# The queries' factors of a decayed attention kernel, taken as the reciprocal of its first scan

## The chip, the cores and the metric

The program runs on one core of a Trainium2 chip. The core has a matrix engine (TensorE, PE in the profile, its weight loads PEld), a vector engine (VectorE, DVE), a scalar engine (ScalarE, ACT), a general engine (GpSimd, POOL) and a queue processor (SyncE, SP), and each runs its own list of instructions in order. They meet through semaphores. On-chip memory is SBUF (128 partitions) and PSUM, into which the matrix engine writes. The metric is the time of one execution on the device, in microseconds. Less is better.

## The reference

Two parts follow each other. The first is a linear attention whose state decays by a factor `alpha` of its own for every key dimension; the second routes each token to one of eight experts.

```python
# q, k, v, alpha: (4, 8, 768, 48) = batch, heads, tokens, head size; alpha between 0.8 and 1.0
for t in range(S):
    state = alpha[:, :, t, :, None] * state + k[t] outer v[t]      # D x D per head
    y[:, :, t] = q[t] applied to state
x = y as (3072 tokens, 384)
logits = x @ w_gate + modality_bias[modality_id]
e_idx = argmax(logits);  gate_w = softmax(logits)[e_idx]
out[token] = gate_w * (relu(x @ w1[e_idx]) @ w2[e_idx])             # 384 -> 1024 -> 384
```

## The kernel before

**Attention in chunks.** The 4 x 768 tokens are cut into 24 chunks of 128 tokens (six a batch). Inside a chunk the recurrence is turned into matrix products: with P(t) the product of all decays after token t up to the chunk's end, each key is multiplied by P(t) and each query by 1/P(t). The product over the whole chunk, A, carries the state from one chunk to the next. Two heads share a tile, so that four pairs (`NP`) lie side by side.

**The decays, lines 225 to 242.** `turn_decay` turns a chunk's alpha with four transposes on TensorE (L222) and copies them to `X` (L227, on ACT but for the first chunk). `X` has four stretches of 128 decays, with a zero column between them (`SEG` = 129). `decay` then runs four VectorE instructions. L235 scans `X` backwards, 516 columns, `G = G * X + DR`; `DR` is 1 at the start of each stretch and 0 elsewhere, so `G` holds the products P(t), and A at columns `1::SEG`. L239 puts A, kept from below by `AFLOOR` = 1e-30, into `amin`. L240 takes its reciprocal, four columns, into `DF`. L241 scans `X` forwards, `Fw = Fw * X + DF`, and so gives the factors 1/P(t) as 1/A times the decays up to t. `amin` is read once, at the end of attention (`out_of_range`, L665), to see if a general way of computing is needed (it is not with these inputs).

**What uses them.** `scale_k` (L257) multiplies the turned keys by `G` into `kh`; `scale_q` (L263) the turned queries by `Fw` into `qh`. `scores` (L272) multiplies `kh` and `qh` on TensorE, ACT copies the result to `scT` (L276), POOL masks it (L277). `keys` turns `kh` back (L286, copied to `knat` by ACT). `combine` multiplies the state `S` by A (`t1`, L299, shown as `t`), copies it in halves to `UB` on ACT (L302), makes `kv` = keys by values (L308), adds it to the state (L311; L313 where a batch begins), and forms the output `y` (L321 from the state, L323 from the scores).

**The order.** The loop at L764 is a software pipeline: in step s it turns the decays of chunk s, scales the keys and queries of chunk s-1, makes the scores of s-2, combines s-3, writes out s-4. Routing of finished groups of tokens is spread over the steps. From step 4 TensorE keeps the order of the program (`pin`); on the other engines a planner that simulates the program chooses the order of the instructions, subject to what they depend on. On ACT the two copies to `UB` are placed ahead of the next step's copy to `X`. PSUM tiles named `tr` have three buffers, used in turn by the three input transposes, `keys` and `rows`.

**Experts.** After attention 12 tiles of 256 tokens run through the experts, plus partial ones (`slot`, `half`), with float32 split in two parts (L863, L865) and three products for each (L891 to L893, L914 to L916).

Of the kernel before, what the change touches and what calls it, by code (L numbers as in the profile page):

```python
# [8 lines left out]
F32 = mybir.dt.float32  # L9
# [5 lines left out]
ALU = mybir.AluOpType  # L15
# [6 lines left out]
P = 128  # L22
B, H, S, D = 4, 8, 768, 48
NC = S // P
NP = H // 2
SEG = P + 1
DM = H * D
E = 8
F = 1024
# [17 lines left out]
AFLOOR = 1.0e-30  # L47
# [5 lines left out]
def attention_moe(ctx: ExitStack, tc: tile.TileContext, q, k, v, alpha, mid, wg, mb, w1, w2, out):  # L53
    nc = tc.nc
    vec, act, pool, pe, sp = nc.vector, nc.scalar, nc.gpsimd, nc.tensor, nc.sync
# [7 lines left out]
    ac = actx.enter_context(tc.tile_pool(name="ac", bufs=1))  # L63
    sb = actx.enter_context(tc.tile_pool(name="sb", bufs=2))
# [10 lines left out]
    for i in range(NB):  # L75
        for n, val in (("a", 1.0), ("k", 0.0), ("q", 0.0)):
            t = ac.tile([P, H, 64], F32, name=f"nat_{n}{i}")
# [4 lines left out]
    for i in range(NV):  # L82
        t = ac.tile([P, H, 64], F32, name=f"vt{i}")
# [11 lines left out]
    st = {}  # L95
# [49 lines left out]


    DR = ac.tile([P, NP * SEG + 1], F32, name="DR")
    vec.memset(DR, 0.0)
    vec.memset(DR[:, SEG :: SEG], 1.0)
    X, DF, UB = [], [], []  # L150
    for i in range(2):
        t = ac.tile([P, NP * SEG + 1], F32, name=f"X{i}")
        vec.memset(t[:, 0 :: SEG], 0.0)
        X.append(t)
        t = ac.tile([P, NP * SEG], F32, name=f"DF{i}")
        vec.memset(t, 0.0)
        DF.append(t)
        t = ac.tile([P, NP, 2, 64], F32, name=f"UB{i}")
        vec.memset(t, 0.0)
        UB.append(t)  # L160
# [3 lines left out]
    amin = ac.tile([P, NU, NP], F32, name="amin")  # L164
# [51 lines left out]
    def seg(t, lo):  # L216
        return t.rearrange("p (a b) -> p a b", b=SEG)[:, :, lo : lo + P]

    def trans(i, n):
        p = ps.tile([P, NP, P], F32, name="tr", bufs=3)  # L220
        for j in range(NP):
            pin(pe.transpose(p[:, j], nat[n, i % NB][:, 2 * j : 2 * j + 2].rearrange("p a b -> p (a b)"), ident))  # L222
        return p
# [5 lines left out]
            mark["X"] = turned  # L229

    def decay(i):
        x, d = X[i % 2], DF[i % 2]
        Fw = sb.tile([P, NP * SEG], F32, name="Fw", bufs=3)
        G = sb.tile([P, NP * SEG + 1], F32, name="G", bufs=4)
        vec.tensor_tensor_scan(  # L235
            G[:, 1:][:, ::-1], x[:, 1:][:, ::-1], DR[:, 1:][:, ::-1], 0.0, op0=ALU.mult, op1=ALU.add
        )
        ac1 = amin[:, i]
        vec.tensor_scalar(ac1, G[:, 1::SEG], AFLOOR, None, op0=ALU.max)  # L239
        vec.reciprocal(d[:, 0::SEG], ac1)  # L240
        vec.tensor_tensor_scan(Fw, x[:, :-1], d, 0.0, op0=ALU.mult, op1=ALU.add)  # L241
        st[i, "G"], st[i, "F"] = G, Fw

    def guard(i):
# [15 lines left out]
    def scale_q(i):  # L260
        qh = sb.tile([P, NP, P], F32, name="qh", bufs=3)
        pq = trans(i, "q")
        vec.tensor_tensor(qh, pq, seg(st[i, "F"], 1), op=ALU.mult)  # L263
        st[i, "q"] = qh

    def scores(i):
# [497 lines left out]
    for s in range(NU + 3):  # L764
# [14 lines left out]
        if 0 <= s - 1 < NU:  # L779
            scale_q(s - 1)  # L780
        if s < NU:
            decay(s)
# [262 lines left out]
```

## Time and profile before

| what | value |
|---|---|
| runs | 430.09, 429.88, 425.59 us; median 429.88 |
| the profiled execution's own time | 424.6 us |
| its span in the trace | 422.9 us |
| mean granted TensorE clock | 0.984 |
| attention's decays run from | 6.3 us (first L235) to 152.8 us (end of the last L241) |
| VectorE instructions | 546, of which 48 are the long scans |

The span runs from the first to the last instruction. In the views, a row of the groups gives line, engine, operation, output and inputs with their shapes, the count, the busy time in all, the mean of one in ns, and the idle time ahead of them with what ended it. In a timeline row the first two numbers are start and length in us, and the bracket holds the idle time ahead and its releaser. A row of waits gives the total, the number and the longest. Consecutive VectorE instructions overlap by some hundredths of a microsecond, so the distance between starts is what one adds to the queue.

### The profile page before, as it was taken

To read this page: it belongs to the slowest core of one execution; us is meant where nothing else is said; L and a number is where in the kernel's file an instruction comes from. 1 tells how busy PE (TensorE), PEld (TensorE's weight loads), DVE (VectorE), ACT (ScalarE), POOL (GpSimd) and SP (SyncE) were. 2 spreads that over 40 slices of the span, in tenths; PEclk is the share of its full clock that TensorE was granted. 3 is DMA by queue.
4 is the path that set the end of the run, shared out by engine and by line. 5 is a ranking of instruction groups with operands and counts; after the bars stand their busy time and mean duration, and the time that the engine had idled before them with its cause. 6 is when DMAs were issued, how large, how long until landed. Compare 5 with 4: busy or idle time off the path is not lost. (4 is left out here: it accounts for less than half of the span.)

```text
span 422.9 us, 9633 instructions
## 1 busy us (share of the span) xinstructions
PE 384.9 (91%) x3659; PEld 356.4 (84%) x3659; DVE 275.4 (65%) x546; ACT 236.3 (56%) x441; POOL 133.0 (31%) x175
## 2 busy tenths in 40 slices
PE   3988998999999888889899999999999999999590
PEld 2777887888778776769799999999999999999590
DVE  6878679777888973488299567565675656622040
ACT  3577677668576555347287556556565565532220
POOL 9222121212212233403557524443352431410100
PEclk9999999999999999999999999999999999999886
DMA  7999688588484087504999966686666865300270
GB/s 147 211 196 215 149 177 167 116 170 185 115 176 108 37 297 265 189 20 153 387 312 370 321 215 212 200 296 205 208 206 205 294 208 170 115 19 21 71 279 6
DMA packets 134489, 78.37 MB, mean 185 GB/s; under 512 B 103809, under 2 KB 121278, under 8 KB 134424
## 3 DMA queue, kind: packets, MB, share of 16 engines
q1 hardware_dynamic: 130328, 67.72, 57.0%
q0 software_dynamic: 4096, 9.85, 6.1%
q8 instruction: 33, 0.54, 0.5%
q14 instruction: 32, 0.26, 0.2%
HBM read 68.10 MB, written 9.65 MB: 184 GB/s over the span
## 5 line engine op out<-in xcount | busy, mean ns | idle before, releaser
L865 DVE TENSOR_TENSOR w2L<-w2r,w2H 128x768 fp32r<-128x768 f32 x52 | 49.0, 957 | 54.1 <-ACT w2H L863 54.1
L891 PE MATMUL tr<-xH,w1H 128*128 128x256 f32 x264 | 75.2, 286 | 0.6 <-issue 0.4
L892 PE MATMUL tr<-xL,w1H 128*128 128x256 f32 x264 | 74.8, 284 | 0.4 <-issue 0.4
L893 PE MATMUL tr<-xH,w1L 128*128 128x256 f32 x264 | 74.6, 283 | 0.3 <-issue 0.3
L277 POOL TENSOR_SCALAR_AFFINE_SELECT scT<-scT 128x512 f32<-128x512 f32 x48 | 32.4, 693 | 115.0 <-ACT scT L276 114.9
L914 PE MATMUL sc<-w2H,hH 128*128 128x384 f32 x192 | 64.4, 338 | 0.0
L915 PE MATMUL sc<-w2L,hH 128*128 128x384 f32 x192 | 63.9, 335 | 0.0
L833 POOL DMA_INDIRECT out_dram<-os,odx x24 | 28.4, 1185 | 111.8 <-ACT os L919 60.9
L916 PE MATMUL sc<-w2H,hL 128*128 128x384 f32 x192 | 62.5, 335 | 0.0
L863 ACT CAST w2H<-w2r 128x768 fp32r<-128x768 f32 x52 | 42.5, 835 | 35.6 <-PE sc L916 29.6
L865 DVE TENSOR_TENSOR w1L<-w1r,w1H 128x768 fp32r<-128x768 f32 x44 | 41.7, 959 | 16.9 <-ACT w1H L863 16.3
L891 PEld LDWEIGHTS tr<-xH,w1H 128*128 128x128 f32 x264 | 50.4, 191 | 1.3 <-issue 1.3
L892 PEld LDWEIGHTS tr<-xL,w1H 128*128 128x128 f32 x264 | 50.5, 191 | 1.0 <-issue 0.9
L863 ACT CAST w1H<-w1r 128x768 fp32r<-128x768 f32 x44 | 36.0, 835 | 26.5 <-PE tr L892 22.2
L893 PEld LDWEIGHTS tr<-xH,w1L 128*128 128x128 f32 x264 | 50.6, 192 | 0.0
L898 DVE SCALAR_TENSOR_TENSOR hL<-tr,hH 128x512 fp32r<-128x512 f32 x46 | 31.5, 686 | 16.6 <-ACT hH L895 13.5
L654 POOL DMA_INDIRECT gg<-gd,idx x26 | 31.5, 1213 | 20.6 <-ACT os L919 8.8
L914 PEld LDWEIGHTS sc<-w2H,hH 128*128 128x128 f32 x192 | 36.1, 188 | 0.5 <-issue 0.5
L895 ACT ACTIVATE hH<-tr 128x512 fp32r<-128x512 f32 x46 | 27.2, 593 | 16.5 <-PE tr L893 9.0
L915 PEld LDWEIGHTS sc<-w2L,hH 128*128 128x128 f32 x192 | 36.1, 188 | 0.0
L916 PEld LDWEIGHTS sc<-w2H,hL 128*128 128x128 f32 x192 | 35.9, 188 | 0.0
L323 PE MATMUL y<-scT,vt 128*64 128x128 f32 x384 | 35.9, 273 | 0.0
(224 smaller groups left out, 750.6 us busy)
## 6 DMA issues: line engine op xcount, KB each, us to landing
w1r<-in_moe_w_dram SPq DMA_DIRECT2D x28, 768.0 KB
w2r<-in_moe_w_dram SPq DMA_DIRECT2D x28, 768.0 KB
nat_a<-in_alpha_dram SPq DMA_DIRECT2D x24, 192.0 KB
nat_k<-in_k_dram SPq DMA_DIRECT2D x24, 192.0 KB
nat_q<-in_q_dram SPq DMA_DIRECT2D x24, 192.0 KB
vt<-in_v_dram SPq DMA_DIRECT2D x24, 192.0 KB
xd<-xs SPq DMA_DIRECT2D x24, 192.0 KB
xg<-xd,idx POOLq DMA_INDIRECT x26
```

What stands on the lines that cost most here:

```text
L277: pool.affine_select(s, s, [[0, NP], [1, P]], ALU.is_ge, 0.0, base=0, channel_multiplier=-1)
L323: pin(pe.matmul(y[r, j], vt[:, 2 * j + g], sc[g][:, j], start=(c == 0), stop=True))
L654: pool.indirect_dma_start(gg[i % NX][:, u : u + 1], None, gd[0:rows], ix, bounds_check=rows - 1, oob_is_err=False)
L863: act.copy(hi, src)
L865: vec.tensor_tensor(lw, src, hi.bitcast(F32), op=ALU.subtract)
L891: pe.matmul(hp[:, z], wH[:, d, fs], xH[:, d], start=(d == 0), stop=False)
L892: pe.matmul(hp[:, z], wH[:, d, fs], xL[:, d], start=False, stop=False)
L893: pe.matmul(hp[:, z], wL[:, d, fs], xH[:, d], start=False, stop=(d == ND - 1))
L898: mark[f"h{j}L"] = vec.scalar_tensor_tensor(hL, hp, 0.0, hH.bitcast(F32), op0=ALU.max, op1=ALU.subtract)
L914: pe.matmul(op, hH[:, z, us], wH[:, z], start=(f == 0), stop=False)
L915: pe.matmul(op, hH[:, z, us], wL[:, z], start=False, stop=False)
L916: pe.matmul(op, hL[:, z, us], wH[:, z], start=False, stop=(f == NF - 1))
```

## The change

The second scan, the small maximum and the small reciprocal go. The first scan now has a maximum as its second operation, with `DR` holding `AFLOOR` in place of 0, so that the floor is kept inside the scan (`G = max(G * X, DR)`; the zero column of `X` and the 1 in `DR` still start each stretch). One reciprocal over all 4 x 128 products gives the queries' factors. The copy of A to `amin` is made by POOL. The two `DF` tiles and their memsets go; `Fw` has 512 columns in place of 516.

```diff
     DR = ac.tile([P, NP * SEG + 1], F32, name="DR")
-    vec.memset(DR, 0.0)
+    vec.memset(DR, AFLOOR)
     vec.memset(DR[:, SEG :: SEG], 1.0)
-    X, DF, UB = [], [], []
+    X, UB = [], []
...
-        t = ac.tile([P, NP * SEG], F32, name=f"DF{i}")
-        vec.memset(t, 0.0)
-        DF.append(t)
...
     def decay(i):
-        x, d = X[i % 2], DF[i % 2]
-        Fw = sb.tile([P, NP * SEG], F32, name="Fw", bufs=3)
+        x = X[i % 2]
+        Fw = sb.tile([P, NP, P], F32, name="Fw", bufs=3)
         G = sb.tile([P, NP * SEG + 1], F32, name="G", bufs=4)
         vec.tensor_tensor_scan(
-            G[:, 1:][:, ::-1], x[:, 1:][:, ::-1], DR[:, 1:][:, ::-1], 0.0, op0=ALU.mult, op1=ALU.add
+            G[:, 1:][:, ::-1], x[:, 1:][:, ::-1], DR[:, 1:][:, ::-1], 0.0, op0=ALU.mult, op1=ALU.max
         )
-        ac1 = amin[:, i]
-        vec.tensor_scalar(ac1, G[:, 1::SEG], AFLOOR, None, op0=ALU.max)
-        vec.reciprocal(d[:, 0::SEG], ac1)
-        vec.tensor_tensor_scan(Fw, x[:, :-1], d, 0.0, op0=ALU.mult, op1=ALU.add)
+        vec.reciprocal(Fw, seg(G[:, 1:], 1))
+        pool.tensor_copy(amin[:, i], G[:, 1::SEG])
         st[i, "G"], st[i, "F"] = G, Fw
...
-        vec.tensor_tensor(qh, pq, seg(st[i, "F"], 1), op=ALU.mult)
+        vec.tensor_tensor(qh, pq, st[i, "F"], op=ALU.mult)
```

## The prediction

> **What bounds the kernel now.** I read the busy time by stretch first, to find the stage that the change lies in and what fills it.
>
> ```profile
> 10.00:150.00 140.00, 130.23 (x1712) 110.94 (x1711) 114.76 (x248) 93.42 (x209) 30.15 (x46) 1.00 0.72 154
> 150.00:210.00 60.00, 52.61 (x542) 44.97 (x542) 35.09 (x129) 27.83 (x54) 21.28 (x22) 1.00 0.61 221
> 210.00:390.00 180.00, 180.00 (x1288) 179.77 (x1287) 113.66 (x146) 105.77 (x165) 69.39 (x58) 1.00 0.63 213
> ```
>
> The columns are the length, then busy time of PE, PEld, DVE, ACT and POOL, the granted clock, the DMA share and GB/s. From 10 to 150 us attention runs: PE is busy 130.2 of 140 us, VectorE 114.8, and so 25.2 us of VectorE and 9.8 us of PE are free. From 210 to 390 us TensorE is busy without a gap in the experts, which start from what attention leaves; there a later start is a later end. So a microsecond that attention gains or loses is, near enough, one of the total. The stage's price is set by its steps, one for each chunk, and next I look at what they wait for.
>
> ```profile
> ACT UB L302 <- DVE t L299: 24.2, 19, 2.7
> PE tr L286 <- ACT X L227: 6.1, 9, 1.6
> ACT X L227 <- PE tr L222: 5.9, 10, 1.4
> ```
>
> ACT stands still 19 times, 24.2 us in all, until VectorE has `t`. PE then waits for the copy of `X` that follows the `UB` copies on ACT; only 10 of the 23 `X` copies wait for PE's transposes. One step shows the ring:
>
> ```profile
> 96.99 1.22 DVE L235 TENSOR_TENSOR_SCAN G<-X,DR 128x516 f32<-128x516 f32 x1
> 98.13 0.67 DVE L263 TENSOR_TENSOR qh<-tr,Fw 128x512 f32<-128x512 f32 x1
> 98.71 0.16 DVE L239 TENSOR_SCALAR amin<-G 128x4 f32<-128x4 f32 x1
> 98.91 0.18 DVE L240 RECIPROCAL DF<-amin 128x4 f32<-128x4 f32 x1
> 99.12 1.23 DVE L241 TENSOR_TENSOR_SCAN Fw<-X,DF 128x516 f32<-128x516 f32 x1
> 100.27 0.33 DVE L313 COPY S<-kv 128x192 f32<-128x192 f32 x1
> 100.64 0.59 DVE L299 TENSOR_TENSOR t<-S,G 128x192 f32<-128x192 f32 x1
> 101.27 0.71 ACT L302 COPY UB<-t 64x192 f32<-64x192 f32 x2 [0.46 <-DVE t L299]
> 102.01 0.58 ACT L227 COPY X<-tr 128x512 f32<-128x512 f32 x1
> 102.65 1.22 DVE L235 TENSOR_TENSOR_SCAN G<-X,DR 128x516 f32<-128x516 f32 x1
> ```
>
> Scan `G`, `qh`, the three instructions for `Fw`, `S`, `t`; then ACT's `UB`, `X`; then the next scan `G`. Each starts within 0.1 us of the end of the one ahead: `UB` ends at 101.98 and `X` starts at 102.01, `X` ends at 102.59 and the scan starts at 102.65. The step is 5.66 us long, and in steps of this kind what is added between L235 and L299 on VectorE lengthens it by its full size, though VectorE has free time elsewhere.
>
> **The change part by part.** *Removed.* From the start of L239 (98.71) to the start of `S` (100.27) the old instructions hold the queue for 1.56 us. That is what goes from each step.
>
> *Added: a reciprocal of 128x512.* The trace has none of that size, but three small ones, and plain instructions beside them:
>
> ```profile
> L240 DVE RECIPROCAL DF<-amin 128x4 f32<-128x4 f32 x24 | 4.3, 178 | 0.6
> L239 DVE TENSOR_SCALAR amin<-G 128x4 f32<-128x4 f32 x24 | 3.8, 160 | 0.0
> L636 DVE RECIPROCAL gt<-sm 128x6 f32<-128x6 f32 x1 | 0.2, 191 | 0.0
> L635 DVE TENSOR_SCALAR sm<-sm 128x6 f32<-128x6 f32 x1 | 0.2, 161 | 0.0
> L636 DVE RECIPROCAL gt<-sm 128x18 f32<-128x18 f32 x1 | 0.2, 247 | 0.0
> 147.58 0.15 DVE L635 TENSOR_SCALAR sm<-sm 128x18 f32<-128x18 f32 x1
> L257 DVE TENSOR_TENSOR kh<-tr,G 128x512 f32<-128x512 f32 x24 | 16.5, 687 | 20.1 <-PE tr L222 20.0
> ```
>
> The plain instruction costs the same for 4, 6 and 18 columns (160, 161, about 150 ns). The reciprocal does not: 178, 191, 247. From 6 to 18 columns it grows by 56 ns, 4.67 a column; from 4 to 18 by 69, 4.93; against the plain instruction of the same width it is (247-150)/18 = 5.4 ns a column dearer. A 128x512 multiplication takes 687 ns in all, or about 1.0 to 1.3 ns a column. So an estimate for 512 columns is 247 + 494 x 4.93 = 2680 ns; the ends of the likely value are 247 + 494 x 4.67 = 2550 and 150 + 512 x 5.4 = 2915. The outer ends are the ordinary instruction, 687 ns, if the slope is a start-up effect, and the steepest pair, (191-178)/2 = 6.5 a column, giving 3460. I take 2.7, as the 4-column value is a mean of 24 and the 18-column one is the widest. The old scan ends at 100.35 and the next instruction starts at 100.27, so 0.08 overlaps, and the reciprocal holds the queue 2.62 us: 2.62 - 1.56 = **1.06 us more a step** (0.91 to 1.27 for the likely ends).
>
> [...]
>
> *The scan with a maximum.* Same columns, still a product and one more operation on the running value; I take the old 1.22 (the gain or loss of another second operation I bound by nothing to +-0.1 us, as L241 and L235 agree to 0.01 here).
>
> *POOL's copy.* One of 4 columns, waiting for `G`. The nearest POOL row:
>
> ```profile
> L179 POOL CAST tok<-ti 128x24 f32<-128x24 int32 x1 | 0.2, 192 | 0.0
> L277 POOL TENSOR_SCALAR_AFFINE_SELECT scT<-scT 128x512 f32<-128x512 f32 x48 | 32.4, 693 | 115.0 <-ACT scT L276 114.9
> ```
>
> Behind it on POOL are the masks, which wait 114.9 us in all for ACT; 24 x 0.2 us lie in that. Without that cover it is at most 4.6 us (24 x 192 ns). `out_of_range` reads `amin` once, after the last reciprocal, when the copy is long done: nothing. The removed `DF` memsets lie ahead of VectorE's first wait for PE, so they gain nothing.
>
> *Where the 1.06 us is paid.* By the 23 copies of `X` and the last chunk:
>
> ```profile
> 24.55 0.58 ACT L227 COPY X<-tr 128x512 f32<-128x512 f32 x1
> 148.78 0.58 ACT L227 COPY X<-tr 128x512 f32<-128x512 f32 x1
> 37.07 0.58 ACT L227 COPY X<-tr 128x512 f32<-128x512 f32 x1 [0.66 <-PE tr L222]
> 122.40 0.59 ACT L227 COPY X<-tr 128x512 f32<-128x512 f32 x1 [0.52 <-PE tr L222]
> 128.83 0.58 ACT L227 COPY X<-tr 128x512 f32<-128x512 f32 x1 [0.30 <-PE tr L222]
> 135.06 0.68 DVE L257 TENSOR_TENSOR kh<-tr,G 128x512 f32<-128x512 f32 x1
> 96.38 0.69 DVE L257 TENSOR_TENSOR kh<-tr,G 128x512 f32<-128x512 f32 x1 [1.46 <-PE tr L222]
> 18.81 1.36 DVE L235 TENSOR_TENSOR_SCAN G<-X,DR 128x516 f32<-128x516 f32 x1 [1.69 <-ACT X L227]
> 153.21 0.17 PE L430 MATMUL rt<-oh,tri 128*128 128x16 bf16 x1 [0.40 <-DVE vals L502]
> ```
>
> Nine copies, of which the first and last rows are the first and last, start 0.02 to 0.03 us after `UB` ended, as at 102.01: full price. The step whose `kh` starts at 135.06 without a wait has a full VectorE: full price. Together 10 x 1.06 = 10.6. Seven have about 0.6 us of slack, a wait for the transposes of 0.52 to 0.66 (rows three and four, first and last of five) or ACT's own guard activation: 7 x 0.46 = 3.2. One has 0.30: 0.76. Two, where a batch begins and no `UB` stands ahead, have an idle VectorE like the 1.46 us at 96.38: nothing. The first three copies of all go together: their chunks add 3 x 1.06 on VectorE before its idle 1.69 at 18.81, which leaves 1.5. In the last, PE's L430 already waits for VectorE's `vals`: 1.06. The sum is 17.1 us; with the likely ends 14 (0.91) and 22 (1.27).
>
> *Contention.* Where POOL's mask and VectorE meet, VectorE is held:
>
> ```profile
> 61.96 1.34 POOL L277 TENSOR_SCALAR_AFFINE_SELECT scT<-scT 128x512 f32<-128x512 f32 x2 [4.00 <-ACT scT L276]
> 61.97 0.83 DVE L299 TENSOR_TENSOR t<-S,G 128x192 f32<-128x192 f32 x1
> ```
>
> Here `t` took 0.83 us, 0.24 more than the 0.59 at 100.64. If the later `t` meets the mask so in each of the ten tight steps, 2.4 us more; if it slips past, a little less than now. I take nothing and keep 2.4 for the range. [...]
>
> **Sum.** The profiled execution took 424.6 us, and this gives 441.6. It lies 5.3 us under the median of 429.88 and 1.0 under the lowest of the three. As two of the three runs stand near 430, I put the 17.1 on the median: **447 us**.
>
> **The rivals.**
> *A cheap reciprocal (faster).* If the growth over 4, 6 and 18 columns is start-up, 512 columns take 0.69 us; it decides from below 1.64 us for one (1.56 + 0.08). Then each step's ring is 0.95 shorter, but PE is nearly full: what comes back is about what PE now loses to `X`, 6.1 us. That is 418.5 in the profile, 424 on the median. Against it: three widths lie on one line. [...] The 247 ns for 18 columns against about 150 for a plain one disagrees.
>
> *Free time covers it.* If the planner puts `X` ahead of `UB` on ACT, or `t` ahead of the reciprocal, the ring opens and only VectorE's own queue counts: 24 x 1.06 = 25.4 us against 25.2 us free, unevenly spread. Only steps with routing work, like that at 135.06, are full; some five pay, +5 us: 430 in the profile, 435 on the median. For it: the planner is free to do so. Against it: it put `UB` first so far, and `kv` for `S` is not there when the reciprocal starts.
>
> *A dear reciprocal.* At 3.46 us each step pays 1.82: 18.2 + 7 x 1.22 + 1.5 + 1.8 + 3.8 = 34 us, 464 on the median.
>
> *No measurable change.* Cover as above, and the loads of the start or a better order after 150 us (PE has 7.4 us free there) take the rest: about 430.
>
> **How the numbers follow.** Forecast 0.60, cheap reciprocal 0.08, cover 0.15, dear 0.12, no change 0.05. About 1% (4.3 us) is what a measurement of this kernel can tell from none. Faster by more: 0.07, the cheap reciprocal without its mildest cases. Within 1%: 0.12, no change, a third or so of cover, and the rest of the cheap one. Slower: 0.81. The range goes from 432 (cover at its mildest) to 462 (forecast with the dear end, contention and the larger part of the dear case), and leaves out the cheap one and the ends of two others. The forecast's own range is 444 to 454.
>
> **What would show it.** Right: a reciprocal group of 24 at 2.5 to 2.9 us; L235 still at 1.22; steps that were 5.66 us at about 6.7; the wait of `UB` for `t` larger, by about 1 us a step; attention's last scan some 16 us later, and the expert stage as long as before. POOL's copies about 0.2 us with no wait behind them. Wrong: a reciprocal under 1.6 us; `X` ahead of `UB` on ACT; VectorE idle gone but the end of attention unmoved; or a changed order in the experts that costs or gives several microseconds by itself.

## The result, and the profile after

The changed kernel takes 447.26 us, median of four runs (445.89 to 451.11), against 429.99 us for the kernel before (425.59 to 430.33): a ratio of 1.0501, 95% interval 1.0441 to 1.056. It is slower by 17 us. The profiled execution has a span of 443.9 us (its own time 445.89), against 422.9 before.

The first question is in which part of the span the time is. The busy times by stretch, cut at the end of the last instruction that makes the queries' factors (columns as before: length, PE, PEld, DVE, ACT, POOL, clock, DMA share, GB/s). The kernel before:

```profile
6.27:152.78 146.51, 135.74 (x1767) 115.40 (x1768) 121.13 (x261) 96.57 (x217) 33.71 (x54) 1.00 0.73 157
152.78:422.89 270.11, 248.06 (x1890) 240.31 (x1887) 151.04 (x275) 137.79 (x223) 93.62 (x83) 0.97 0.59 202
```

The changed kernel:

```profile
6.17:173.70 167.53, 144.54 (x1751) 121.97 (x1751) 154.92 (x206) 97.75 (x218) 34.57 (x80) 0.97 0.64 139
173.70:443.90 270.20, 250.31 (x1904) 242.72 (x1904) 151.44 (x282) 137.07 (x221) 91.84 (x81) 0.96 0.59 201
```

The stretch behind attention is as long as before: 270.1 and 270.2 us. All 21.0 us of the difference between these two executions lie between the first scan and the last reciprocal. There VectorE was busy 121.1 of 146.5 us, with 25.4 free; now it is busy 154.9 of 167.5, with 12.6 free. So 33.8 us of work came to VectorE, 12.8 of them went into time that was free, and 21.0 made the stage longer.

The groups of the changed kernel that the change touches (VectorE's and POOL's):

```profile
L235 DVE RECIPROCAL Fw<-G 128x512 f32<-128x512 f32 x24 | 80.2, 3343 | 0.0
L232 DVE TENSOR_TENSOR_SCAN G<-X,DR 128x516 f32<-128x516 f32 x24 | 29.4, 1226 | 3.4 <-ACT X L224 3.4
L294 DVE TENSOR_TENSOR t<-S,G 128x192 f32<-128x192 f32 x20 | 7.1, 355 | 0.4
L236 POOL COPY amin<-G 128x4 f32<-128x4 f32 x24 | 4.5, 189 | 93.6 <-DVE G L232 93.6
```

One reciprocal takes 3.34 us. The scan with a maximum costs what the scan with an addition did, and POOL's copy is 0.19 us long and waits for nothing but `G`. One step of the changed kernel, in order of time:

```profile
37.10 1.23 DVE L232 TENSOR_TENSOR_SCAN G<-X,DR 128x516 f32<-128x516 f32 x1 [0.26 <-ACT X L224]
38.37 3.35 DVE L235 RECIPROCAL Fw<-G 128x512 f32<-128x512 f32 x1
40.70 1.22 POOL L272 TENSOR_SCALAR_AFFINE_SELECT scT<-scT 128x512 f32<-128x512 f32 x2 [2.11 <-ACT scT L271]
41.64 0.29 DVE L306 TENSOR_TENSOR S<-t,kv 128x192 f32<-128x192 f32 x1
41.97 0.36 DVE L294 TENSOR_TENSOR t<-S,G 128x192 f32<-128x192 f32 x1
42.36 0.71 ACT L297 COPY UB<-t 64x192 f32<-64x192 f32 x2 [1.25 <-DVE t L294]
43.10 0.59 ACT L224 COPY X<-tr 128x512 f32<-128x512 f32 x1
43.99 1.22 DVE L232 TENSOR_TENSOR_SCAN G<-X,DR 128x516 f32<-128x516 f32 x1
```

From the start of the reciprocal (38.37) to the start of `S` (41.64) are 3.27 us, where the three old instructions took 1.56: 1.71 us more. The ring is the one of the prediction, `t`, `UB`, `X`, next scan. Yet the step, from scan to scan, is 6.89 us long, and the same step of the kernel before (31.45 to 38.12) was 6.67. And not every step is built so any more:

```profile
73.74 0.59 ACT L224 COPY X<-tr 128x512 f32<-128x512 f32 x1 [0.95 <-PE tr L219]
74.83 0.72 ACT L297 COPY UB<-t 64x192 f32<-64x192 f32 x2
```

Here `X` stands ahead of `UB` on ACT and waits for PE's transposes, not for `t`. It is so in five steps of the changed kernel and was so in none before: with the longer instruction the planner chose another order. In four further steps, those with routing work, it moved `t` ahead of most of the routing instructions. The same step (to the scan of the nineteenth chunk) in the kernel before, and then in the changed one:

```profile
114.38 0.95 DVE L451 TENSOR_TENSOR OL<-ioh,lo 128x768 f16<-128x768 f16 x1
115.25 0.35 DVE L299 TENSOR_TENSOR t<-S,G 128x192 f32<-128x192 f32 x1
```

```profile
130.62 0.36 DVE L294 TENSOR_TENSOR t<-S,G 128x192 f32<-128x192 f32 x1
131.18 0.95 DVE L446 TENSOR_TENSOR OL<-ioh,lo 128x768 f16<-128x768 f16 x1
```

Before, `UB` and `X` could start only when the routing work (`OL` and others) was done; now they run beside it. The step was 7.43 us long and is 7.52.

### The profile page after: what moved, and what is told of

Same layout as the page of the kernel before. It is cut to its first block, busy times and chain, and to the rows that moved or that the text cites. A ratio compares the mean times of both kernels' runs of the same rounds, so it can differ in the third digit from the quotient of the medians.

```text
span 443.9 us, 9627 instructions
## 1 busy us (share of the span) xinstructions
PE 395.9 (89%) x3659; PEld 365.4 (82%) x3659; DVE 308.6 (70%) x496; ACT 236.7 (53%) x441; POOL 131.9 (30%) x199
## 5 line engine op out<-in xcount | busy, mean ns | idle before, releaser
L235 DVE RECIPROCAL Fw<-G 128x512 f32<-128x512 f32 x24 | 80.2, 3343 | 0.0
L828 POOL DMA_INDIRECT out_dram<-os,odx x24 | 27.5, 1146 | 112.1 <-ACT os L914 61.8
L858 ACT CAST w1H<-w1r 128x768 fp32r<-128x768 f32 x44 | 36.0, 835 | 25.4 <-PE tr L887 21.3
L272 POOL TENSOR_SCALAR_AFFINE_SELECT scT<-scT 128x512 f32<-128x512 f32 x48 | 29.5, 635 | 43.5 <-ACT scT L271 43.5
L318 PE MATMUL y<-scT,vt 128*64 128x128 f32 x384 | 38.7, 288 | 0.0
L649 POOL DMA_INDIRECT gg<-gd,idx x26 | 31.4, 1210 | 18.9 <-ACT os L914 8.5
```

Source lines behind the costliest of these rows:

```text
L235: vec.reciprocal(Fw, seg(G[:, 1:], 1))
L318: pin(pe.matmul(y[r, j], vt[:, 2 * j + g], sc[g][:, j], start=(c == 0), stop=True))
L649: pool.indirect_dma_start(gg[i % NX][:, u : u + 1], None, gd[0:rows], ix, bounds_check=rows - 1, oob_is_err=False)
L858: act.copy(hi, src)
```

## The experiments

The kernel before has its own median beside each set: 426.34 us for the first four, 427.29 for the second, 426.15 for the third.

**The second scan put back.** The rest of the change stays.

```diff
-        vec.reciprocal(Fw, seg(G[:, 1:], 1))
+        vec.reciprocal(d[:, 0::SEG], G[:, 1::SEG])
+        vec.tensor_tensor_scan(Fw, x[:, :-1], d, 0.0, op0=ALU.mult, op1=ALU.add)
         pool.tensor_copy(amin[:, i], G[:, 1::SEG])
```

> The changed kernel with the second scan put back: the floor stays in the first scan, POOL keeps the copy of the chunk's product, VectorE takes the four-column reciprocal straight from the scan's result and scans a second time; only the wide reciprocal is gone. Theory (all of the loss is the wide reciprocal holding VectorE's queue): the time falls to that of before or a little under it, 424 to 430 us, since one instruction of 0.16 us a chunk is saved. Rival (part of the loss comes from the rest of the change, the scan with a maximum or the copy on POOL): it stays at 433 us or more.

Measured: 425.01 us (419.10 to 428.65), against 426.34 (422.91 to 430.22). The whole loss is gone with the wide reciprocal; the maximum inside the scan and the copy on POOL cost nothing that can be measured. Whether the 0.16 us a chunk is saved, four runs that spread over 9.6 us can't tell; in the profiled execution the last second scan ended at 150.96 us, 1.8 us earlier than before.

**The reciprocal in four pieces.**

```diff
-        vec.reciprocal(Fw, seg(G[:, 1:], 1))
+        for j in range(NP):
+            vec.reciprocal(Fw[:, j], seg(G[:, 1:], 1)[:, j])
```

> The changed kernel with its reciprocal as four instructions of 128 columns. Theory (cost by column, and part of the loss is short instructions of routing standing behind one long reciprocal): each piece takes about 0.9 us (0.16 + 128 x 6.2 ns), the four together no less than the one, but the short instructions get in between, so that PE's waits for the modality table (3.0 us) and for the first early tile (4.5 us) shrink; 440 to 446 us. Rival (only VectorE's total work counts): as the changed kernel or up to 3 us slower, 447 to 450 us.

Measured: 449.77 us, ratio 1.0583 (1.0496 to 1.067), as the rival had it. The group of the pieces:

```profile
L236 DVE RECIPROCAL Fw<-G 128x128 f32<-128x128 f32 x96 | 81.3, 908 | 0.1
```

The price of a piece is as expected; the gain from letting short instructions in between is not there. PE still waited 4.7 us for the early tile's instruction and 2.8 us for the modality table: the planner mostly left the pieces side by side. So this run gives the price by column, but doesn't tell whether the order matters.

**The modality table's copy on ACT.** In the changed kernel one short copy (`mt`, in `bias_table`) stood behind a reciprocal, PE waited 2.96 us for it, and then ran at a lower clock, 0.52 and 0.62 in two stretches of 4 us. PE's row and the stretches around it, of the changed kernel:

```profile
49.28 1.09 PE L303 MATMUL kv<-vt,knat 128*64 128x48 f32 x16 [2.96 <-DVE mt L198]
```

```profile
44.00:48.00 4.00, 2.31 (x27) 1.92 (x25) 4.00 (x5) 3.41 (x9) 1.30 (x3) 1.00 1.05 228
48.00:52.00 4.00, 2.72 (x34) 2.73 (x36) 3.06 (x9) 0.70 (x2) 0.10 (x1) 0.52 0.03 8
52.00:56.00 4.00, 3.87 (x30) 3.30 (x26) 0.53 (x1) 1.07 (x2) 0.00 (x0) 0.62 0.25 49
```

```diff
-        vec.tensor_copy(mt, mp)
+        act.copy(mt, mp)
```

> The changed kernel with one copy of the modality table moved from VectorE to ACT, so that it doesn't stand behind a reciprocal. Theory (PE's wait of 3.0 us for it and the half clock of PE after it cost time that is not made up): 441 to 444 us, and a full clock around 48 to 56 us. Rival (VectorE's queue alone sets the pace, and the wait is made up later): 446 to 448 us.

Measured: 442.75 us, ratio 1.0444 (1.0355 to 1.0534), in the range of the theory and 3 us below that of the rival. The clock is 1.00 in that stretch of this kernel:

```profile
44.00:60.00 16.00, 13.95 (x209) 12.08 (x207) 14.41 (x19) 10.23 (x25) 3.86 (x8) 1.00 0.60 136
```

The median is 4.5 us lower than the changed kernel's, but the ratios' intervals overlap. By steps, from scan `G` to scan `G`: the one with the wait is 7.82 us long in place of 12.09 (7.78 before the change), so 4.3 us are gone there. Yet the last reciprocal ends only 1.5 us earlier (172.16 against 173.70). Most of that came back in an earlier step, 10.63 us in place of 6.99, which the edit does not touch. There PE's matmuls were still slow in this execution. Four transposes of the changed kernel, and the same four in this one:

```profile
26.02 0.66 PE L281 MATMUL tr<-ident,kh 128*128 128x128 f32 x4
```

```profile
27.31 1.12 PE L281 MATMUL tr<-ident,kh 128*128 128x128 f32 x4
```

The kernel before and the changed one start with such slow matmuls too: 1.09 and 1.08 us for the first four transposes. They ended at about 25 us in the changed kernel's profile and at about 32 us in this one; until 24.9 us this one agrees with the profile of a later kernel that has the same edit (`after_stalls`), where they ended at 25 us and both steps are short (7.20 and 7.83 us). So the wait and its half clock cost 4.3 us of that step, and how much of this reaches the total is not settled.

**A filler of the same size in the kernel before.** A reciprocal of 256 columns that nobody reads, written behind the second scan.

```diff
         vec.tensor_tensor_scan(Fw, x[:, :-1], d, 0.0, op0=ALU.mult, op1=ALU.add)
+        vec.reciprocal(pad[:, :256], G[:, 1:257])
```

> The kernel before with one more reciprocal of 256 columns a chunk after the second scan, whose result nobody reads: about 0.16 + 256 x 6.2 ns = 1.75 us more of VectorE's queue a chunk, as in the changed kernel (1.71), with everything else as before. Theory (the loss is VectorE's added queue time, however it arises): 442 to 450 us. Rival (the loss hangs on who waits for the reciprocal, namely the queries' factors and what was moved): under 438 us, as the filler is behind the factors. Rival (every added microsecond is paid, as the ring through UB and X would have it): 424.6 + 31 or more, over 456 us.

Measured: 451.85 us, ratio 1.0634 (1.0563 to 1.0705), 25.5 us above the kernel before. It is 1.9 us over the range of the theory and outside both rivals' ranges. But the filler did not run where it was written. One chunk:

```profile
114.91 0.16 DVE L240 TENSOR_SCALAR amin<-G 128x4 f32<-128x4 f32 x1
114.98 1.75 DVE L243 RECIPROCAL pad<-G 128x256 f32<-128x256 f32 x1
116.64 0.12 DVE L241 RECIPROCAL DF<-amin 128x4 f32<-128x4 f32 x1
116.80 1.46 DVE L242 TENSOR_TENSOR_SCAN Fw<-X,DF 128x516 f32<-128x516 f32 x1
```

In all 24 chunks, and so too with 64 columns, the planner put it ahead of the small reciprocal and the second scan, so that the queries' factors do stand behind it. The first rival, that the loss hangs on who waits, is therefore not tested by these two runs. **The same with 64 columns:**

> The kernel before with a reciprocal of 64 columns a chunk whose result nobody reads: about 0.16 + 64 x 6.2 ns = 0.56 us, 13 us of VectorE in all, a third of the 256-column filler. Theory (part is filled into VectorE's free time, part is paid in the tight steps): 430 to 434 us, that is +4 to +8. Rival (the free 25 us takes it all up, and only work beyond it costs): within 2 us of before. Rival (every microsecond is paid): +13, about 439 us.

Measured: 432.85 us, ratio 1.0149 (1.0022 to 1.0276): 5.6 us more, in the range of the theory, though not by its sum. It expected 13 us more of VectorE's queue; the filler partly fills the gaps between the short instructions around it, and from `amin` to the second scan a chunk went from 0.41 to 0.69 us only (1.89 with 256 columns). The fillers' groups, of the kernels with 256 and with 64 columns:

```profile
L243 DVE RECIPROCAL pad<-G 128x256 f32<-128x256 f32 x24 | 41.9, 1746 | 0.0
```

```profile
L243 DVE RECIPROCAL pad<-G 128x64 f32<-128x64 f32 x24 | 13.1, 547 | 0.0
```

And the stretch of the decays in each, cut as above:

```profile
6.28:178.51 172.23, 146.40 (x1767) 123.39 (x1768) 155.56 (x287) 97.55 (x218) 40.80 (x56) 0.99 0.62 138
```

```profile
6.61:158.08 151.47, 140.13 (x1767) 118.14 (x1768) 127.92 (x285) 97.36 (x219) 36.41 (x50) 1.00 0.71 153
```

Against the kernel before (146.51 us, VectorE 121.13), 34.4 us more of VectorE made the stage 25.7 us longer, and 6.8 us more made it 5.0 longer: 75 and 73 in a hundred are paid. In the changed kernel it is 21.0 for 33.8, or 62 in a hundred. So VectorE time that makes nothing costs about as much as that of the wide reciprocal, and not every microsecond of it is paid. The shares are of one execution each and no constant: with 256 columns 8.3 of the 25.7 us lie in the third and fourth step (9.47 and 10.76 us against 5.61 and 6.35), where PE's matmuls stayed slow until 34 us, against 13 in the kernel before.

**The ring opened.** `UB` copied by POOL in place of ACT, so that `X` is not behind `t`.

```diff
-                act.copy(U[r, :, g, :D], t1[r])
+                pool.tensor_copy(U[r, :, g, :D], t1[r])
```

> The kernel before with the two copies to UB of each chunk made by POOL in place of ACT, so that ACT's copy of X no longer stands behind VectorE's t. Theory (the ring t, UB, X, scan sets the step before the change, in 10 of 23 steps): steps of the tight kind get shorter, and the time falls by 3 to 8 us, to 418 to 424. Rival (PE sets the step and the ring only looks tight): within 2 us of before.

Measured: 428.77 us, ratio 1.005 (0.9997 to 1.0103). The total is in the rival's range. The last second scan, though, ended at 148.37 us in place of 152.78, and the time came back behind it. The waits of POOL in this kernel show where to look:

```profile
POOL UB L302 <- DMA gg<-gd,idx: 5.0, 2, 4.4
POOL UB L302 <- DMA xg<-xd,idx: 4.9, 1, 4.9
```

The last chunks' copies stand on POOL behind the indirect gathers of the first expert tiles. So in three further kernels POOL copies `UB` for chunks 0 to 18 only:

```diff
-                act.copy(U[r, :, g, :D], t1[r])
+                (pool.tensor_copy if i < 19 else act.copy)(U[r, :, g, :D], t1[r])
```

> The kernel before with UB copied by POOL for chunks 0 to 18 and by ACT for the last five, whose copies on POOL stood behind indirect gathers (waits of 4.4 and 4.9 us). Theory (the ring through UB and X did set the tight steps, and what POOL won in attention was lost behind its gathers): the last second scan ends near 148 us as with POOL throughout, against 152.8 before, and the total falls by 3 to 5 us. Rival (PE sets the pace; the earlier end of the scans is only VectorE running ahead): total within 2 us of before.

Measured: 421.99 us, ratio 0.9876 (0.9831 to 0.9921), 4.2 us less: the ring did set some steps. The other half of the expectation was not met: in the profiled execution (425.45 us, above the median) the last scan ended at 153.0 us, not near 148. In that execution the granted clock was 0.50 from 20 to 28 us and 0.65 from 44 to 48, and the two steps there took 9.73 and 9.38 us, against 6.60 and 7.73 with `UB` on POOL throughout. Less these 4.8 us the scan would have ended near 148, an estimate; so that half is open.

> The changed kernel with UB copied by POOL for chunks 0 to 18. Theory (VectorE's queue is nearly full, 155 of 167 us, and the ring adds the rest): 440 to 444 us, a few us below the changed kernel. Rival (the ring through UB is the whole loss, as the prediction's sum had it): 432 to 436 us. Rival (VectorE alone): 446 to 448 us.

Measured: 444.18 us, ratio 1.0421 (1.0359 to 1.0484), against 1.0501 for the changed kernel. That is at the upper end of the theory's narrow range (0.2 us over it) and far from the rival by which the ring is the whole loss. As the two intervals overlap, a gain of about 3 us is likely and not certain. Set beside the kernel before with the same `UB` (421.99), it is 22.2 us longer: with the ring opened in both kernels the loss is no smaller than with it closed.

> The second scan put back, the floor in the first scan and the product's copy on POOL as in the changed kernel, and UB copied by POOL as well. Theory (the ring sets the tight steps; two small savings add up): 416 to 422 us, faster than both kernels. Rival (PE sets the step): 424 to 427 us, as with the second scan alone.

Measured: 423.89 us, ratio 0.9922 (0.9876 to 0.9967). It lies between the two ranges, and above the theory's.

> Second scan put back, floor in the first scan, the product's copy on POOL, UB on POOL for chunks 0 to 18. Theory (both savings of attention are kept): 417 to 421 us. Rival (PE sets the pace): 423 to 425 us, as with UB on POOL throughout.

Measured: 420.70 us (415.82 to 423.56, twelve runs), ratio 0.9851 (0.9809 to 0.9893), in the range of the theory. It is the lowest median here, 1.5% below the kernel before; its interval overlaps that of the kernel before with the same `UB`, so that the gain from the rest is not certain. Its last second scan:

```profile
145.28 1.22 DVE L239 TENSOR_TENSOR_SCAN Fw<-X,DF 128x516 f32<-128x516 f32 x1
```

It ends at 146.5 us, 6.3 before the old one.

**A wait at the end of attention.** PE waited 4.5 us in the changed kernel for a short instruction of the first early tile (L528) that stood behind the last chunk's reciprocal. With the table's copy on ACT as above, and:

```diff
-        vec.reciprocal(Fw, seg(G[:, 1:], 1))
+        with issue_after("ohe0" if i == NU - 1 else None):
+            vec.reciprocal(Fw, seg(G[:, 1:], 1))
```

where `ohe0` marks that instruction.

> The changed kernel with the modality table's copy on ACT and the last chunk's reciprocal queued behind the short instruction (OHE) for which PE waited 4.5 us. Theory (short instructions that PE waits for, standing behind a long reciprocal, are a part of the loss beside VectorE's total): 436 to 440 us, below the 442.75 of the table's copy alone. Rival (the delay at the end is VectorE's backlog, and is only moved): 442 to 444 us.

Measured: 443.59 us, ratio 1.0443 (1.0343 to 1.0543), the same as without this edit. PE's waits before, in the changed kernel, and in this one:

```profile
PE rt L541 <- DVE OHE L528: 4.5, 1, 4.5
```

```profile
PE rt L426 <- DVE vals L498: 3.0, 1, 3.0
PE rt L542 <- DVE OHE L529: 0.8, 1, 0.8
```

The 4.5 us fell to 0.8, and 3.0 us appeared at the next instruction that PE needs from the same queue. The total is in the rival's range: this change of order only moved the wait. That VectorE's backlog is behind it fits, but no other order was tried.

**A cheap instruction in the reciprocal's place.** The queries' factors are not computed in this one, so that routing and the experts' share of work differ; only attention is compared.

```diff
-        vec.reciprocal(Fw, seg(G[:, 1:], 1))
+        vec.tensor_tensor(Fw, seg(G[:, 1:], 1), seg(G[:, 1:], 1), op=ALU.mult)
```

> The changed kernel with a 128x512 multiplication (G by G) in place of the reciprocal: the queries' factors are not computed, so that routing and the experts' work differ and only attention is compared. One instruction of about 0.69 us in place of 3.34. Theory (price of the rival with a cheap reciprocal: up to 6 us): the last of these instructions ends 3 to 6 us before the 152.8 us at which the last second scan ended before. Rival (PE sets the pace): within 1 us of 152.8 less the length of what is gone.

Its last such instruction:

```profile
149.21 0.68 DVE L235 TENSOR_TENSOR Fw<-G 128x512 f32<-128x512 f32 x1
```

It ends at 149.9 us, 2.9 before the 152.8 of the old scan, a little under the range. So even with a reciprocal as cheap as a multiplication the change would have brought about 3 us of attention, in this one execution. PE's matmuls were slow again there from 17 to 20 us (its third step took 7.01 us against 5.61), so that it may be more.

## Why the prediction held, and where its steps failed

The total came out as forecast, 447 us, but two steps of the sum were wrong in opposite directions, and that they cancel to 0.3 us is luck.

- **The reciprocal's duration was mis-sized.** It was put at 2.7 us, with 2.55 to 2.9 as likely ends, and is 3.34: 1.71 us more a step, not 1.06. The slope was taken between 4 or 6 and 18 columns (4.7 to 4.9 ns a column). The runs give 547, 908, 1746 and 3343 ns for 64, 128, 256 and 512 columns, which is 5.6, 6.5 and 6.2 ns a column between neighbours. The steepest small pair (6.5) would have been nearly right; it was kept as the outer end, 3.46, and the truth lies beside that end, in the rival of a dear reciprocal.
- **The rule for what is paid, full price in ten steps, failed.** By the prediction's list of steps 1.71 us would cost 10 x 1.71 + 7 x 1.11 + 1.41 + 1.71 + (3 x 1.71 - 1.69) = 31.4 us. The two profiled executions differ by 21.0 us. Step by step, from scan `G` to scan `G`, the difference lies elsewhere than forecast:

| steps as the prediction sorted them | cost by its list, at 1.71 us | cost in the profiles, us |
|---|---|---|
| nine with `X` right behind `UB` (full price) | 15.4 | 3.3 |
| the one with a full VectorE (full price) | 1.7 | 0.9 |
| seven with about 0.6 us of slack | 7.8 | 9.4 |
| the one with 0.30 us of slack | 1.4 | 0.8 |
| two where a batch begins | 0 | 0.5 |
| the first three | 3.4 | 4.0 |
| behind the last scan `G` | 1.7 | 2.2 |

The nine tight steps paid 0.09 to 0.64 us each, not 1.71. All five steps in which the planner put `X` ahead of `UB` are among them, the step at 102.01 that the prediction shows too (5.66 us before, 6.19 now), and so are the four in which it moved `t` ahead of routing work. The prediction had named `X` ahead of `UB` as a sign of being wrong, and this opening of the ring is the condition of its rival "Free time covers it". In these nine steps VectorE is now busy for 93 to 100 in a hundred of the time: its queue bounds them, and no longer the ring. Of the 9.4 us of the seven, 6.3 lie in two steps, 12.09 us for 7.78 and 8.37 for 6.43, in which PE's granted clock fell (0.52 and 0.62 in the stretches from 48 to 56 us, 0.65 from 100 to 104); the first is the one with the wait for `mt`. With the wide reciprocal the loss is as large when `UB` is on POOL in both kernels (22.2 us), so it does not need the ring. The ring is real but small: taking it away makes the kernel before 1.2% faster.
- **Contention went the other way.** The prediction allowed up to 2.4 us of loss where `t` meets POOL's masks. `t` became shorter, 355 ns against 415, and short routing instructions shrank much more. The 0.59 us from which the prediction counted a meeting was one itself: two masks ran from 100.39 to 101.73, and `t` alone takes 0.36. Two lines, of the kernel before and of the changed one:

```profile
L413 DVE TENSOR_TENSOR ls<-L,mx 128x32 f32<-128x32 f32 x2 | 1.1, 548 | 0.0
```

```profile
L408 DVE TENSOR_TENSOR ls<-L,mx 128x32 f32<-128x32 f32 x2 | 0.4, 191 | 0.1
```

The instruction is the same. Before, one of the two (133.31, 0.56 us) ran beside masks (132.61 to 134.41) and the other (173.41, 0.54 us) beside an indirect gather of POOL (172.93 to 173.93); now the masks run beside the reciprocal (in the step above from 40.70 to 41.92, all but the last 0.2 us before the reciprocal ends at 41.72). Such shorter instructions are most of the reason why VectorE's busy time grew by 33.8 us and not by 24 x 1.71 = 41. That the meeting is the cause is read from the times, and was not tried by itself.
- **Where the sum was put.** 17.1 us were added to the median because the profiled execution of before was a low one. It was: profile to profile the difference is 21.0, median to median 17.3. The agreement of 17.1 with 17.3 rests on this too. (424.6 and 17.1 make 441.7, where the prediction has 441.6.)
- **Right:** the loss is that of the wide reciprocal alone (without it 425.0 us); the scan with a maximum and POOL's copy cost nothing that can be measured, and the first scan starts at 6.17 us against 6.27, so that the removed memsets bring next to nothing; the stage after attention is as long as before. Attention ended 21 us later where 16 were forecast.
- **Not decided:** how much of the total the two waits of PE behind a long reciprocal, and the lower clock after them (0.50 from 49 to 55 us and from 176 to 180), cost. Taking one of them away made its step 4.3 us shorter in two kernels, and their medians are 442.75 and 443.59 us, with intervals that overlap the changed kernel's. And whether the loss hangs on who waits for the reciprocal: the fillers ran ahead of the second scan, so no run here tells.

## What to carry to other kernels

An instruction's price at full width should be taken from the steepest of the small samples, or measured, when all the samples are far smaller than the case: here 18 columns gave 4.9 ns a column and 512 columns 6.2. An engine that is four fifths busy has free time in the average only: of the time added to its queue 62 to 75 in a hundred came through here. A step that is tight in the old profile is tight in the old order: with the longer instruction the planner moved what could move, and nine such steps paid 3.3 us in place of 15.4. So compare the steps one by one, and look where the planner put an instruction before an experiment with it is read. Work on a critical ring that another engine can do is worth moving, but not behind that engine's waits for transfers: the same move was worth nothing with the last chunks on POOL and 1.2% without them.

## What the runs showed of the hardware

- The reciprocal of VectorE costs 6.2 ns for each float32 column from 256 to 512 columns, against 1.3 for a multiplication of 512 columns, all in (687 ns). Cutting it in four costs next to nothing by itself: the four, of 908 ns each, overlap at their starts and took 3.39 us in a step where they stood side by side, against 3.34 for the one.
- While a reciprocal ran from SBUF to SBUF, POOL's masks ran at full speed. All masks of the kernel before, then all of the changed one (shortest, median and longest in ns):

```profile
L277 POOL TENSOR_SCALAR_AFFINE_SELECT scT<-scT x48: 629/636/1218, 15.2 to 173.9; 128x512 f32<-128x512 f32 x48
```

```profile
L272 POOL TENSOR_SCALAR_AFFINE_SELECT scT<-scT x48: 629/634/652, 17.8 to 197.1; 128x512 f32<-128x512 f32 x48
```

The longest, 1218 ns, started beside a second scan (132.61, with the scan from 132.18 to 133.40); beside the reciprocals none takes over 652. In the kernel before, the five pairs of masks that began with more than 0.3 us of a second scan still to run (28.16, 40.85, 81.72, 120.16 and 132.61) took 1.46 to 1.80 us, and the pairs beside no scan 1.22 to 1.34. The scan reads two inputs and the reciprocal one; whether that makes the difference was not tried.
- TensorE's granted clock fell to about half after two waits in the changed kernel. After the one of 2.96 us at 49.28 it was 0.52 and 0.62 in the stretches from 48 to 56 us, against 1.00 from 44 to 48. After one of 1.73 us at 97.95, in a stretch with PE busy for 2.27 of 4 us, it was 0.65 from 100 to 104.
- Four transposes take 1.04 to 1.12 us on TensorE at the start of an execution and 0.60 to 0.66 later, and the clock column shows 1.00 for both in the kernel before and the changed one. The change came at about 13 us in the kernel before, 25 in the changed one, 34 with the filler of 256 columns, and at 25 or 32 us in two kernels that agree until 24.9 us. So a stage's length in one profile can differ by some microseconds for this alone: 10.63 against 7.20 us in one step of these two.
